# First loads of a sum of a state-space layer and a gated MLP: K tile 0 and x tile 2 moved from ScalarE's DMA queue to SyncE's

## The chip, the cores and the metric

The kernel runs on one core of one Trainium2 chip. The metric is device time in microseconds of one execution. The kernel before takes 177.66 us (median of 3 runs, 177.61 to 177.72).

A core has five engines with instruction queues of their own: TensorE (PE in the profile, its weight loads PEld), VectorE (DVE), ScalarE (ACT), GpSimd (POOL) and SyncE (SP, which here only starts transfers). Transfers between the chip's memory and the on-chip memory are started from the queue of an engine and carried out by 16 DMA engines. Engines wait for each other, and for transfers, by semaphores.

## What is computed

The input x has 2048 rows of 512. A layer norm comes first, then two branches read the normed rows xn, and the output is x plus both:

```python
def _A_ref(x, Lambda_re, Lambda_im, B_re, B_im, C_re, C_im, log_dt, Dskip):
    Lam = Lambda_re + 1j * Lambda_im
    dt = jnp.exp(log_dt)
    Lam_bar = jnp.exp(dt * Lam)
    B_bar = ((Lam_bar - 1.0) / Lam)[:, None] * (B_re + 1j * B_im)
    Bu = jnp.einsum("bld,pd->blp", x + 0j, B_bar)
    for t in range(L):
        h = Lam_bar[None, :] * h + Bu[:, t, :]
    y = 2.0 * jnp.einsum("blp,dp->bld", hseq, Cmat).real + x * Dskip[None, None, :]
def _B_ref(x, w_gate, w_up, w_down):
    return (_silu(x @ w_gate) * (x @ w_up)) @ w_down
xn = _layernorm(x, axis=-1)
return x + _A_ref(xn, ...) + _B_ref(xn, ...)
```

w_gate and w_up are 512 x 1376, w_down is 1376 x 512, B and C are 512 x 512. Everything in memory is bfloat16.

## The kernel before

**Tiling.** The 2048 rows are 16 x tiles of 128 rows, in four chunks of four. The hidden width of 1376 is ten tiles of 128 and a rest of 96; the inner dimension of 512 is four K tiles of 128. For each chunk TensorE computes the gate and up products two hidden tiles at a time (lines 721, 764), ScalarE takes them out of PSUM (silu in line 733, a copy in line 799), and VectorE multiplies them (line 802). TensorE also computes Bu (line 849), VectorE rotates it and runs the recurrence as scans along the rows (lines 880 and 889). At the end come the down product (line 918), the product with C that is added to it (line 932), and an addition on VectorE with the store (line 936). PSUM is used as four pairs of banks, taken in turn.

**The start.** Chunk 0 is normed tile by tile (`ln_chunk0`, lines 514 to 528): statistics of an x tile (518, 519), its standard deviation on ScalarE (520), the reciprocal (525) and the norm (501). All of it is tied into one fixed order on VectorE, and the transpose of the small parameters (523) stands in that order ahead of the reciprocal of tile 3. TensorE transposes each normed tile (549), and ScalarE (560), for tile 3 VectorE (558), moves it to xnT. The first seven hidden tiles of the gate product of chunk 0 are computed in quarters, a quarter being the 128 rows of one x tile, and within a quarter K tile by K tile (line 764, `ffn_gate_quarters`). So seven matmuls need only K tile 0, the next seven K tile 1, and so on. The eighth hidden tile (number 7, `NQ`) follows as a whole in line 775, then the up products.

**The loads.** The first seven hidden tiles of w_gate (896 columns, `FG`) come as four loads, one for each K tile (`wg_load`, 224 KB each); the columns from 896 on come in one load, ld_wg1 (line 442, 480 KB), which hidden tile 7 also needs (`wres`, line 706). w_up comes in two (ld_wu0 and ld_wu1). The x tiles 0 to 3 come singly (`x_load`, 128 KB each), then four at a time. `ld_touch` is a read of 64 bytes. Three parameter rows (`pload`) follow the last single x tile.

**The order.** Work is declared as tasks with reads and writes. A planner (`_schedule`) walks through them with estimated durations and fixes the order of each engine's stream. TensorE's and SyncE's tasks keep the order in which they are declared (`_CHAIN`); ScalarE's, VectorE's and GpSimd's are ordered by the planner's priorities, within extra ordering edges written by hand. For a transfer the planner counts on a rate for each starting queue, which for ScalarE's is half that of SyncE's. A transposing load (`xpose=True`, for instance B_re in line 447) waits for every transfer declared before it, except those named in `beside`, and every later transfer waits for it; so the transfers from ld_bre on follow one another.

**At the top of the queues.** SyncE starts x tiles 0 and 1, K tiles 1, 2, 3, x tile 3, the three parameter rows, then ld_wu0, ld_wg1, ld_wu1 and ld_x4. ScalarE starts ld_touch, K tile 0 and x tile 2, and then loads its activation table with a first small operation, which has an ordering edge behind the last task of `act_q`.

Of the kernel before, what the change touches and what calls it, by code (L numbers as in the profile page):

```python
# [250 lines left out]
def bass_parallel_sum__ssm_conv_s5__swiglu_ffn__prompt_kernel(  # L251
# [32 lines left out]
    with es:  # L284
# [112 lines left out]
        def dma(name, dst, src, writes, nbytes, reads=(), after=(), out_=False, eng="sp", xpose=False, prio=0.0, order=(), beside=(), **kw):  # L397
            after = tuple(after)
            if xpose:
                after = after + tuple(t for t in dma_tasks if t.name not in beside)  # L400
                fn = lambda e, dst=dst, src=src: e.dma_start_transpose(out=dst, in_=src)
                est, nb = 1900.0, int(nbytes * 1.2) + 140000
            else:
                if xp_state[0] is not None:
                    after = after + (xp_state[0],)
                fn = lambda e, dst=dst, src=src: e.dma_start(dst, src, **kw)
                est, nb = 330.0 + nbytes / 900.0, nbytes
            t = g.add(eng, fn, reads=reads, writes=writes, name=name, dma=True, after=after, out=out_, est=est, nbytes=nb, prio=prio, order=order)
            dma_tasks.append(t)
            if xpose:  # L410
                xp_state[0] = t
            return t
# [9 lines left out]
        def x_load(a, **kw):  # L422
            return dma("ld_x%d" % a, x_sb[:, a:a + 1, :], x_v[:, a:a + 1, :], [("x", a)], TILEB, **kw)

        def wg_load(nm, k0, k1, **kw):
            return dma("ld_wg" + nm, wg[:, k0:k1, 0:FG], wg_v[:, k0:k1, 0:FG], [("wg", nm)], (k1 - k0) * 128 * FG * 2, **kw)
# [2 lines left out]
        x_load(0)  # L429
        x_load(1)  # L430
        act_q = [dma("ld_touch", tch[0:16, 0:1], wg_v[0:128:8, 0:1, 0:2], [("tch",)], 16 * 4, eng="act")]
        act_q.append(wg_load("k0", 0, 1, eng="act", order=(act_q[-1],)))
        act_q.append(x_load(2, eng="act", order=(act_q[-1],)))
        wg_load("k1", 1, 2)
        wg_load("k2", 2, 3)
        wg_load("k3", 3, 4)
        x_load(3)
        pload("ld_ldt", 2, A_log_dt)
# [624 lines left out]
```

## Time and profile before

| what | value |
|---|---|
| median of 3 runs | 177.66 us (177.61 to 177.72) |
| the profiled execution, its time | 177.57 us |
| its span, first to last instruction | 175.6 us |
| TensorE matmuls | busy 172.5 us, 98% of the span |
| VectorE | busy 161.5 us, 92% |
| ScalarE | busy 83.3 us, 47% |
| GpSimd | busy 10.6 us, 6% |
| granted TensorE clock | 1.0 throughout |
| DMA | 13.69 MB, 78 GB/s over the span |

The first eight loads, by the timeline of the two queues and the DMA view of each issue alone:

| load | KB | queue | issued at (us) | issue to landing (us) |
|---|---|---|---|---|
| x tile 0 | 128 | SyncE | 0.78 | 2.1 |
| K tile 0 | 224 | ScalarE | 1.23 | 3.2 |
| x tile 2 | 128 | ScalarE | 1.71 | 3.7 |
| K tile 1 | 224 | SyncE | 1.70 | 3.5 |
| K tile 2 | 224 | SyncE | 2.17 | 3.9 |
| K tile 3 | 224 | SyncE | 2.64 | 4.0 |
| x tile 3 | 128 | SyncE | 3.12 | 3.8 |

x tile 1 is the second of the two transfers that SyncE starts from 0.78 us on. Landing is the time at which the last part of a transfer has counted up its semaphore. Times in the views are from the start of the span. A line of the timeline gives the start, the time from the first to the last of the merged instructions, engine, line of the kernel, operation and how many there are; the bracket behind it, if any, is the idle time of the engine before it and what ended it. PEclk, the granted clock, is the third number from the end in the rows of the windows.

### The profile page before, as it was taken

What the parts mean: (1) busy time and instruction counts of PE and PEld (TensorE: products, weight loads), DVE (VectorE), ACT (ScalarE), POOL (GpSimd) and SP (SyncE); (2) the same over time, 40 slices, a digit from 0 to 9 for tenths busy, and PEclk for the clock granted to TensorE, in tenths of its full rate; (3) what the DMA queues carried; (4) which work ended last, traced back from release to release, by engine and by line L of the source; (5) the groups of instructions that cost most, each with busy time, mean ns of one, the idle gap of its engine ahead of it and who ended that gap; (6) DMA issues with size and microseconds to landing.
All of it is one profiled execution on the core that took longest, in us unless ns stands there. A gap on an engine that the chain in (4) does not pass through costs nothing.

```text
span 175.6 us, 2523 instructions
## 1 busy us (share of the span) xinstructions
PE 172.5 (98%) x978; PEld 84.7 (48%) x978; DVE 161.5 (92%) x279; ACT 83.3 (47%) x113; POOL 10.6 (6%) x21
## 2 busy tenths in 40 slices
PE   7899999999999999999999999999999999999995
PEld 2894444444444495444444444444444444444443
DVE  2873999999999999999999999999999999999933
ACT  4479799899999766697560000000265620000000
POOL 3040500217000000000000000000000000000000
DMA  4898665645695102300311000022100000000122
GB/s 161 272 385 186 119 118 168 141 107 101 119 300 117 27 0 60 63 0 13 101 39 28 4 0 0 0 90 93 60 0 0 0 0 0 4 0 0 60 91 90
DMA packets 27143, 13.69 MB, mean 78 GB/s; under 512 B 19356, under 2 KB 27004, under 8 KB 27132
## 3 DMA queue, kind: packets, MB, share of 16 engines
q1 hardware_dynamic: 26812, 13.18, 29.0%
q10 hardware_dynamic: 320, 0.36, 0.6%
q8 instruction: 7, 0.11, 0.3%
q14 instruction: 4, 0.03, 0.1%
HBM read 6.85 MB, written 2.10 MB: 51 GB/s over the span
## 4 chain that ended last, share of the span: by engine, by line
PE 96%; DMA 1%; DVE 1%; ACT 0%; issue 0%
PE pb L721 36%; PE pb L918 20%; PE pb L932 16%; PE pb L849 16%; PE pb L764 4%; PE pb L814 3%; PE pb L957 2%; DMA x_sb<-in_A_x_dram 1%; PE pb L549 1%; DVE st L518 0%; DVE xn_sb L501 0%; ACT xnT L560 0%; DVE x_sb L936 0%; ACT sd L520 0%; DVE mv L519 0%
## 5 line engine op out<-in xcount | busy, mean ns | idle before, releaser
L721 PE MATMUL pb<-xnT,wgu 128*128 128x512 bf16 x212 | 46.2, 379 | 0.0
L889 DVE TENSOR_TENSOR_SCAN rot<-sm,car,rot 128x512 bf16<-128x512 f32 x32 | 39.2, 1267 | 0.1
L733 ACT ACTIVATE sg<-pb 128x1024 bf16<-128x1024 f32 x20 | 20.1, 1021 | 39.5 <-PE pb L721 38.4
L721 PEld LDWEIGHTS pb<-xnT,wgu 128*128 128x128 bf16 x212 | 20.7, 98 | 24.8 <-ACT sg L733 0.2
L932 PE MATMUL pb<-W,hss 128*128 128x512 bf16 (+2 forms) x136 | 28.2, 367 | 0.0
L918 PE MATMUL pb<-wd,hT 128*128 128x512 bf16 (+2 forms) x130 | 26.4, 363 | 0.0
L799 ACT ACTIVATE uf<-pb 128x1024 bf16<-128x1024 f32 x20 | 20.5, 1025 | 6.5 <-PE pb L721 4.9
L849 PE MATMUL pb<-xnT,BT 128*128 128x512 bf16 x96 | 21.0, 379 | 0.0
L932 PEld LDWEIGHTS pb<-W,hss 128*128 128x128 bf16 x136 | 12.7, 98 | 15.3 <-issue 0.8
L918 PEld LDWEIGHTS pb<-wd,hT 128*128 128x128 bf16 x130 | 12.3, 98 | 14.0
L856 ACT ACTIVATE u_sb<-pb 128x1024 bf16<-128x1024 f32 x16 | 16.4, 1024 | 5.5 <-PE pb L849 5.2
L721 PE MATMUL pb<-scrC,wgu 128*128 128x512 bf16 x80 | 17.4, 379 | 0.0
L849 PEld LDWEIGHTS pb<-xnT,BT 128*128 128x128 bf16 x96 | 9.4, 98 | 11.4
L936 DVE TENSOR_TENSOR x_sb<-pb,x_sb 128x512 bf16<-128x512 f32 (+2 forms) x17 | 10.7, 645 | 4.0 <-PE pb L932 4.0
L721 PEld LDWEIGHTS pb<-scrC,wgu 128*128 128x128 bf16 x80 | 7.8, 98 | 9.2
L802 DVE TENSOR_TENSOR hT<-sg,uf 128x1024 bf16<-128x1024 bf16 x15 | 10.1, 681 | 0.1
L485 DVE BATCH_NORM_STATS2 st<-x_sb 128x6 f32<-128x512 bf16 x12 | 7.4, 678 | 2.9 <-DMA x_sb<-in_A_x_dram 2.9
L880 DVE TENSOR_TENSOR rot<-u_sb,cosT 128x2048 bf16<-128x2048 bf16 x8 | 9.8, 1220 | 0.0
L880 DVE TENSOR_TENSOR rot<-u_sb,sin 128x2048 bf16<-128x2048 bf16 x8 | 9.7, 1218 | 0.0
L880 DVE TENSOR_TENSOR rot<-rot,sin 128x2048 bf16<-128x2048 bf16 x8 | 9.7, 1217 | 0.0
L880 DVE TENSOR_TENSOR rot<-rot,cosT 128x2048 bf16<-128x2048 bf16 x8 | 9.7, 1211 | 0.0
L880 DVE TENSOR_TENSOR hss<-rot 128x2048 bf16<-128x2048 bf16 x8 | 9.6, 1218 | 0.0
(85 smaller groups left out, 161.6 us busy)
## 6 DMA issues: line engine op xcount, KB each, us to landing
out_dram<-x_sb SPq DMA_DIRECT2D x15, 128.0 KB, 1.7
x_sb<-in_A_x_dram SPq DMA_DIRECT2D x3, 512.0 KB, 4.6
wd<-in_B_w_down_dram SPq DMA_DIRECT2D x1, 1280.0 KB, 6.4
wgu<-in_B_w_up_dram SPq DMA_DIRECT2D x1, 768.0 KB, 4.7
wgu<-in_B_w_gate_dram SPq DMA_DIRECT2D x3, 224.0 KB, 3.9
wgu<-in_B_w_up_dram SPq DMA_DIRECT2D x1, 608.0 KB, 6.7
wgu<-in_B_w_gate_dram SPq DMA_DIRECT2D x1, 480.0 KB, 5.6
x_sb<-in_A_x_dram SPq DMA_DIRECT2D x3, 128.0 KB, 2.9
```

Source lines behind the costliest of these rows:

```text
L485: return g.add("dve", lambda e, a=a: e.bn_stats(out=st[:, a % 8, :], in_=x_sb[:, a, :]), reads=[("x", a)], writes=[("st", a % 8)], name="b ...
L721: inst = e.matmul(pbank[0:fs, bk, :].rearrange("p (j t) -> p j t", j=4), lhsT=w[:, kt, i * 128:i * 128 + fs], rhs=xnT[c][:, :, kt, :], sta ...
L733: g.add("act", lambda e: e.activation(out=sg[rows, sl, 0:n, :].rearrange("p a t -> p (a t)"), in_=pair_f32(rows, bk, 512 * n), func=AF.Sil ...
L799: g.add("act", lambda e: e.activation(out=uf[rows, ul, 0:n, :].rearrange("p a t -> p (a t)"), in_=pair_f32(rows, bk, 512 * n), func=AF.Ide ...
L802: g.add("dve", lambda e: e.tensor_tensor(out=hT_pair(c, i0), in0=sg[rows, sl, 0:n, :], in1=uf[rows, ul, 0:n, :], op=ALU.mult), reads=[("sg ...
L849: inst = e.matmul(pbank[:, bk, :].rearrange("p (j t) -> p j t", j=4), lhsT=BT[:, ri, kt, pt * 128:(pt + 1) * 128], rhs=xnT[c][:, :, kt, :] ...
L856: g.add("act", lambda e: e.activation(out=u_sb[:, us].rearrange("p r t -> p (r t)"), in_=pair_f32(slice(0, 128), b0), func=AF.Identity), r ...
L880: tt = lambda out, a, b, op, r, w, nm: g.add("dve", lambda e: e.tensor_tensor(out=out, in0=a, in1=b, op=op), reads=r, writes=w, name="%s_% ...
L889: g.add("dve", lambda e, A0=A0, A1=A1, k=k, ri=ri, pt=pt: e.tensor_tensor_scan(out=A1[:, k, ri, :], data0=rr[:, pt:pt + 1].to_broadcast([1 ...
L918: inst = e.matmul(pbank[:, bk, 0:nc_], lhsT=hT_pair(c, i - i % 2)[:, i % 2, lt * 128:(lt + 1) * 128], rhs=wd[:, i, c0:c0 + nc_], start=(i ...
L932: inst = e.matmul(pbank[:, bk, 0:nc_], lhsT=hss[:, hb, pt, ri, lt * 128:(lt + 1) * 128], rhs=W12[:, ri, pt, c0:c0 + nc_], start=False, sto ...
L936: g.add("dve", lambda e: e.tensor_tensor(out=x_sb[:, a, c0:c0 + nc_], in0=pbank[:, bk, 0:nc_], in1=x_sb[:, a, c0:c0 + nc_], op=ALU.add), r ...
```

## The change

K tile 0 and x tile 2 are no longer started by ScalarE, whose queue keeps ld_touch alone. SyncE starts x tiles 0 and 1, K tiles 0, 1 and 2, x tile 2, K tile 3 and x tile 3, one behind the other, and then everything else as before. The ordering edge of ScalarE's table load goes to ld_touch, the last task of `act_q` that is left. Nothing else is edited; sizes, buffers and the work of the other engines are the same, and the planner runs anew over the changed list of tasks.

```diff
         x_load(0)
         x_load(1)
         act_q = [dma("ld_touch", tch[0:16, 0:1], wg_v[0:128:8, 0:1, 0:2], [("tch",)], 16 * 4, eng="act")]
-        act_q.append(wg_load("k0", 0, 1, eng="act", order=(act_q[-1],)))
-        act_q.append(x_load(2, eng="act", order=(act_q[-1],)))
-        wg_load("k1", 1, 2)
-        wg_load("k2", 2, 3)
+        for k in range(3):
+            wg_load("k%d" % k, k, k + 1)
+        x_load(2)
         wg_load("k3", 3, 4)
         x_load(3)
         pload("ld_ldt", 2, A_log_dt)
```

## The prediction

> **What bounds the kernel now.** I read the page's shares first (TensorE busy for 98% of the span, VectorE 92%), then the chain of waits in order of time:
>
> ```profile
> 0.78 2.14 DMA x_sb<-in_A_x_dram
> ...
> 5.39 1.18 PE pb L764 x18
> ...
> 12.62 11.22 PE pb L721 x52
> ...
> 173.02 0.43 PE pb L918 x10
> ```
>
> Columns: start, length, work. The first x tile's transfer, its norm on VectorE and the first transposes end in gate matmuls at 5.39 us; from there to 173.8 us the chain is TensorE almost without a break. So the change can gain little: only what comes ahead of 5.39 us. It can lose wherever a load arrives after the time at which TensorE asks for it, and every such loss reaches the end. As the matmuls stand back to back, two late loads don't add: the end moves by the larger lateness. So I compare each load with its due time.
>
> The timeline of SyncE's queue (start, time taken, transfer):
>
> ```profile
> 0.78 0.87 SPq L406 DMA_DIRECT2D x_sb<-in_A_x_dram  x2
> 1.70 1.38 SPq L406 DMA_DIRECT2D wgu<-in_B_w_gate_dram  x3
> 3.12 0.43 SPq L406 DMA_DIRECT2D x_sb<-in_A_x_dram  x1
> 3.59 0.74 SPq L406 DMA_DIRECT2D prow<-in_A_log_dt_dram  x1
> ...
> 5.54 0.44 SPq L406 DMA_DIRECT2D wgu<-in_B_w_up_dram  x1
> 6.03 0.50 SPq L406 DMA_DIRECT2D wgu<-in_B_w_gate_dram  x1
> ```
>
> Three K tiles take 1.70 to 3.12, so one issue costs 0.47 us of the queue; one x tile 3.12 to 3.59, also 0.47. The transfer at 6.03 is ld_wg1. The DMA issues started around 6.03, taken alone, give its landing (KB, then us):
>
> ```profile
> wgu<-in_B_w_gate_dram SPq DMA_DIRECT2D x1, 480.0 KB, 5.6
> ```
>
> It lands at 11.63. Its first reader is not the fifth gate pair at 18.7 us but `ffn_mm(0, NQ, "g", ...)` in line 775: tile 7 begins at column 896, where the K tiles end. The weight loads on TensorE give its due time:
>
> ```profile
> 12.41 0.58 PEld L721 LDWEIGHTS pb<-xnT,wgu 128*128 128x128 bf16 x4
> ```
>
> These are tile 7's four. It has 12.41 - 11.63 = 0.78 us to spare, the smallest cover on the queue behind the moved issues.
>
> **The two moved issues.** SyncE takes K tile 0 and x tile 2: 2 x 0.47 = 0.94 us more of its queue. K tiles 0, 1, 2 go out at 1.70, 2.17, 2.64, x tile 2 at 3.12, K tile 3 at 3.59, x tile 3 at 4.06, and the three parameter loads, ld_wu0, ld_wg1, ld_wu1 and ld_x4 each 0.94 later. ScalarE's table load starts near 1.25, not 2.19; nothing comes of it, as its first real work (3.89) waits for VectorE.
>
> **The eight first loads.** The windows of DMA (last two columns: share of the engines, GB/s):
>
> ```profile
> 2.42:3.00 0.58, 0.58 (x3) 0.24 (x2) 0.05 (x1) 0.58 (x1) 0.00 (x0) 1.00 0.45 146
> 3.00:5.00 2.00, 1.53 (x10) 0.65 (x9) 1.66 (x5) 0.97 (x3) 0.00 (x0) 1.00 1.03 362
> 5.00:6.20 1.20, 1.11 (x20) 0.88 (x18) 0.86 (x4) 0.92 (x4) 0.00 (x0) 1.00 1.02 383
> 7.20:8.00 0.80, 0.80 (x18) 0.80 (x16) 0.49 (x3) 0.61 (x3) 0.00 (x0) 1.00 0.72 182
> 8.00:9.00 1.00, 1.00 (x22) 0.97 (x19) 0.96 (x4) 0.29 (x3) 0.00 (x0) 1.00 1.01 372
> ```
>
> The engines are full from 3.0 to 6.2 us, and from 5.0 on SyncE's queue alone (q10 has no packet left) fills them at 383 GB/s. I take it that one queue also fills them from 3.0. By 3.0 some 0.22 MB had moved (0.92 us at 144 and 0.58 at 146 GB/s). Going through the new order with 0.131 MB for an x tile and 0.229 for a K tile, the last bytes pass at 3.8 (K0), 4.4, 5.0, 5.4 (x2), 6.0 (K3), 6.3. K tile 3 has the same bytes ahead of it in both kernels and landed at 2.64 + 4.0 = 6.64, so 0.67 after its last byte; adding this to all: K0 4.4, K1 5.1, K2 5.7, x2 6.0, K3 6.64, x3 7.0. Due times: K0 5.39; K1 seven matmuls of 0.056 later (28 take 1.56 in the chain), 5.78; K2 6.17; K3 three matmuls after the weights at 6.56, 6.73; x2 6.35 (third BATCH_NORM_STATS2); x3 8.06. All are in time, K3 by 0.09 us only. Cost 0. If the queue fills the engines later, K3 pays first. Upper bound: between 2.42 and 2.98 the queue delivered 68 packets, which would make 1.05 us of each tile, against 271 packets per us in 5.0 to 6.2; I take the latter, nearest in load.
>
> **ld_wg1.** 0.94 later is 12.57, and a wait's end reaches the weight load 0.05 later (xn_sb ends at 4.74, TensorE starts at 4.79): 12.62 - 12.41 = 0.21 us of wait. Bounds: what precedes ld_wg1 on the engines is ld_wu0, which starts slowly: 39 GB/s from 6.6 to 7.2, 182 to 8.0, then 372. The 0.17 MB moved by 8.0 are worth 0.46 us at full rate, so it runs as if full from 7.54, 2.0 us after its issue. Likewise x tiles 8 to 11 (issued 27.37; 92 GB/s from 28.4 to 29.0, then 370) come to 1.48 us, and w_down (issued 47.35) to 1.77. With 1.48 instead of 2.0, ld_wg1 lands at 12.05 and nothing waits. I take 2.0: the same transfer after the same pause. On the far side, were each added issue as slow as the 0.74 us at 3.59, it lands 0.53 later: 0.74 us of wait.
>
> A rule of the Trainium skill goes against this term. "DMA: Bandwidth & Descriptors", section "Issuing engines are not separate DMA queues", says that transfers started from several engines share the same 16 DMA engines, so that a second starter saves only issue time, usually small beside the transfer. By the rule the sum would be 0, as in the first rival. The trace agrees that 0.94 us is small beside 5.6, but not beside a cover of 0.78.
>
> **The rest of the queue.** ld_wu0 lands at 5.54 + 4.7 = 10.24, then 11.2; its matmuls follow tile 7's. The parameter loads' landings aren't shown; the last is issued at 4.97, then 5.91, its transpose due at 8.89. At the 2.0 us of the small read on ScalarE's queue it has 1 us left; a later one would hold xn3 and the transposes at 10.06. ld_wu1 lands at 6.58 + 6.7 = 13.28, and the transpose load of B_re waits for it (issue 13.29, 4.6 us), then B_im (17.95, 4.3 us, landing 22.3). B_im's weights are due four matmuls after those at 23.47: 24.33. With 0.94 more it lands at 23.2, 1.1 us in hand. ld_x4 lands at 15.98 and VectorE, idle for 2.94 us, starts on it at 16.00:
>
> ```profile
> 16.00 2.47 DVE L485 BATCH_NORM_STATS2 st<-x_sb 128x6 f32<-128x512 bf16 x4 [2.94 <-DMA x_sb<-in_A_x_dram]
> ...
> 157.79 2.35 DVE L880 TENSOR_TENSOR hss<-rot 128x2048 bf16<-128x2048 bf16 x2
> ```
>
> From there it has no idle time until 167 us, so all its work moves 0.94. The last hss pair is ready at 160.14, then 161.1; its first reader follows 32 matmuls of 0.216 after 159.42, at 166.3. VectorE's idle ends near the end (0.99, 1.04, 1.03 us) take up the rest. In the middle, hmul0_0 (18.67) queues behind these statistics and releases ScalarE's buffer for the copy at 19.41, done at 20.43; its PSUM bank is due at 23.85. Cost 0, with 2.4 us or more in hand each. The planner may reorder VectorE and ScalarE a little, as its transfer times move too; the same covers pay.
>
> **Sum.** 0.21 us at line 775, nothing else: 177.57 (profiled: 175.6 of span and 1.97 around it) + 0.21 = 177.78. The median of the runs, 177.66, is 0.09 above the profiled execution, so I forecast 177.87. About 0.2% (0.36 us) is what a measurement of this kernel can tell from no change; the forecast is inside it.
>
> **The rivals.**
> - ld_wg1 in time: ld_wu0 starts up as the loads at 27 and 47 us did, because its first slow stretch belonged to the moment. 177.66. Against it: that stretch is this very transfer's.
> - Slower, one queue doesn't keep the first stage fed or keep its pace: K tile 3, x tile 2 or ld_wg1 land 0.4 to 0.9 us after their due times. It decides from 6.73 us for K3 (cover 0.09), 12.41 for ld_wg1. For it: 146 GB/s between 2.42 and 3.0 with queued work; against: 383 GB/s later. Middle 0.65: 178.3.
> - Slower by the transposes: ld_x4's landing takes 8.9 us, though the engines fall from 356 GB/s (12.6 to 13.8) to 73 (13.8 to 14.5): a last piece straggled some 1.5 us. If in the new time that hits ld_wu1, B_re starts at 13.29 + 0.94 + 1.5 = 15.7 and B_im lands at 24.7 against 24.33: 0.4 us, 178.06.
> - Faster: x tile 0, freed of ScalarE's transfers, lands sooner; the 128 KB stores take 1.7 us against its 2.14, so up to 0.44. It pays only if ld_wg1 is in time as well: 12.05 + 0.05 leaves 0.31 of it, 177.35. Against: K tile 0 was issued 0.45 us after x tile 0, and nearly all traffic on ScalarE's queue falls after 2.92.
>
> **How the numbers follow.** Chances: forecast 0.42, ld_wg1 in time 0.14, the first stage or the queue's pace 0.22, the transposes 0.14, faster 0.08. Within 0.2%: the rival in time and most (0.34) of the forecast's case, 0.48. Slower: 0.08 of the forecast's own spread up to 0.74, 0.22 and 0.14, 0.44. Faster 0.08. The likeliest case alone spans 177.7 to 178.4; the range 177.5 to 178.5 leaves out most of the faster case and the first stage's worst.
>
> **What would show it.** Right: the weight load of line 721 after the gate quarters starts near 12.6, with idle time ended by the w_gate transfer; SyncE issues ld_wu0 at 6.48; TensorE starts on L764 at 5.39 still; ld_x4 lands near 16.9. Wrong: idle time of TensorE at 6.7 (K3) or 24.3 (B_im), first matmuls away from 5.39, or tile 7 on time.

## The result, and the profile after

| kernel | median of its runs | lowest to highest | runs |
|---|---|---|---|
| before | 177.61 us | 177.42 to 178.23 | 17 |
| after | 178.38 us | 177.75 to 178.87 | 17 |

The ratio is 1.0042, 95% interval 1.0033 to 1.0052: the change costs 0.75 us, more than the 0.2% that can be told from nothing. The forecast was 177.87 us and the range 177.5 to 178.5, so the range holds the median, but the likeliest case is not what happened: the case of the first stage (second rival, middle 178.3) is. The range held because that rival was in it, not by the sum. The profiled execution of the changed kernel took 178.41 us, with a span of 176.6 us (175.6 before), at a granted clock of 1.0.

The chain of waits of the changed kernel (start, length, work), which before went back to the first x tile:

```profile
3.59 4.16 DMA wgu<-in_B_w_gate_dram
7.75 0.05 issue
7.80 0.73 PE pb L763 x10
...
13.65 11.22 PE pb L720 x52
24.87 13.81 PE pb L848 x64
```

(The line numbers of the changed kernel are smaller by 1.) The chain now goes back to a weight load: K tile 3, issued at 3.59, landed at 7.75. Before, line 721's 52 matmuls began at 12.62 in this view, now at 13.65: 1.03 us later, and the span is 1.0 longer. So all of this execution's loss is there before 8 us, and nothing behind it changes it.

The timeline of TensorE's weight loads in the changed kernel (the bracket is idle time before the group and what ended it):

```profile
5.42 0.95 PEld L763 LDWEIGHTS pb<-xnT,wgu 128*128 128x128 bf16 x14 [0.20 <-ACT xnT L559]
6.87 0.24 PEld L763 LDWEIGHTS pb<-xnT,wgu 128*128 128x128 bf16 x4 [0.50 <-issue]
...
7.79 0.56 PEld L763 LDWEIGHTS pb<-xnT,wgu 128*128 128x128 bf16 x10 [0.41 <-DMA wgu<-in_B_w_gate_dram]
```

The gate matmuls start at 5.42 (5.39 before). After 14 of them, seven for each of K tiles 0 and 1, TensorE is idle for 0.50 us, and again for 0.41 us before the first that needs K tile 3. The trace puts the first gap down to "issue"; the matmul side of the same stop (6.90) names the load of w_gate. Together 0.91 of the 1.0 us (the matmul side, whose ends are modelled, counts 0.35 and 0.24).

How long the loads took, from the view of the DMA issues, each taken alone (KB, then us from issue to landing): K tile 2 (issued 2.65), x tile 2 (3.12) and K tile 3 (3.59).

```profile
wgu<-in_B_w_gate_dram SPq DMA_DIRECT2D x1, 224.0 KB, 4.1
x_sb<-in_A_x_dram SPq DMA_DIRECT2D x1, 128.0 KB, 4.0
wgu<-in_B_w_gate_dram SPq DMA_DIRECT2D x1, 224.0 KB, 4.2
```

| load | due (prediction) | landing forecast | measured | late |
|---|---|---|---|---|
| K tile 1 | 5.78 | 5.1 | 4.9 | no |
| K tile 2 | 6.17 | 5.7 | 6.76 | 0.6 |
| x tile 2 | 6.35 | 6.0 | 7.16 | 0.8 |
| K tile 3 | 6.73 | 6.64 | 7.75 | 1.0 |

The issue times are those of the forecast to 0.01 us. It is the transfers that are late. The windows (the last two columns: busy share of the DMA engines, GB/s), first of the kernel before, then of the changed one:

```profile
3.00:3.60 0.60, 0.60 (x3) 0.20 (x2) 0.60 (x1) 0.59 (x2) 0.00 (x0) 1.00 1.01 356
3.60:4.40 0.80, 0.73 (x4) 0.25 (x2) 0.46 (x4) 0.38 (x2) 0.00 (x0) 1.00 1.01 356
4.40:5.80 1.40, 0.91 (x13) 0.69 (x14) 1.12 (x3) 0.65 (x4) 0.00 (x0) 1.00 1.05 381
```

```profile
2.42:3.00 0.58, 0.58 (x3) 0.24 (x2) 0.08 (x1) 0.39 (x2) 0.00 (x0) 1.00 0.90 258
3.00:3.60 0.60, 0.60 (x3) 0.20 (x2) 0.60 (x1) 0.00 (x0) 0.00 (x0) 1.00 0.78 245
3.60:4.40 0.80, 0.80 (x4) 0.29 (x2) 0.46 (x4) 0.20 (x1) 0.00 (x0) 1.00 1.01 365
4.40:5.80 1.40, 1.24 (x11) 0.83 (x10) 1.09 (x3) 0.66 (x4) 0.00 (x0) 1.00 0.82 195
```

With the 146 GB/s that the prediction shows for 2.42 to 3.0 us, the kernel before moved 0.58 MB from 2.42 to 4.4 us and the changed one 0.59 MB: it is ahead in the first window, behind in the second and level at 4.4 us. The loss is made from 4.4 to 5.8 us, where it moves 1.4 x (381 - 195) = 0.26 MB less. At 380 GB/s that is 0.7 of the 1.1 us by which K tile 3 lands later (7.75, 6.67 before); these rows don't account for the rest. The landings show the same place: K tile 1 lands 0.3 us sooner than before, K tile 2 only 1.85 us after it (0.8 before), and x tile 2 and K tile 3 again 0.4 and 0.6 us apart.

### The profile page after: what moved, and what is told of

It reads as the page before. It is cut to its first block, busy times and chain, and to the rows that moved or that the text cites. A ratio compares the mean times of both kernels' runs of the same rounds, so it can differ in the third digit from the quotient of the medians.

```text
span 176.6 us, 2516 instructions
## 1 busy us (share of the span) xinstructions
PE 172.6 (98%) x970; PEld 85.2 (48%) x978; DVE 161.7 (92%) x279; ACT 83.4 (47%) x113; POOL 10.2 (6%) x21
## 4 chain that ended last, share of the span: by engine, by line
PE 94%; DMA 2%; SPq 1%; issue 1%; DVE 0%
PE pb L720 36%; PE pb L917 19%; PE pb L848 16%; PE pb L931 16%; PE pb L763 3%; PE pb L813 3%; DMA wgu<-in_B_w_gate_dram 2%; PE pb L956 2%; SPq L406 1%; PE pb L548 0%; DVE x_sb L935 0%; PE pb L928 0%
## 5 line engine op out<-in xcount | busy, mean ns | idle before, releaser
L931 PE MATMUL pb<-W,hss 128*128 128x512 bf16 (+2 forms) x132 | 27.6, 366 | 0.4 <-issue 0.3
L879 DVE TENSOR_TENSOR rot<-rot 128x2048 bf16<-128x2048 bf16 x8 | 9.6, 1216 | 0.0
```

The costliest lines, as they stand in the source:

```text
L879: tt = lambda out, a, b, op, r, w, nm: g.add("dve", lambda e: e.tensor_tensor(out=out, in0=a, in1=b, op=op), reads=r, writes=w, name="%s_% ...
L931: inst = e.matmul(pbank[:, bk, 0:nc_], lhsT=hss[:, hb, pt, ri, lt * 128:(lt + 1) * 128], rhs=W12[:, ri, pt, c0:c0 + nc_], start=False, sto ...
```

## The experiments

Two explanations had to be told apart. The first: one queue with all eight loads starves the first stage (theory A). The second: the moved issues delay everything behind them on SyncE's queue, and some cover there breaks. The planner's new order is a third suspect: by the traces at least 79 positions on VectorE and 24 on ScalarE hold another instruction than before. Here is what each run gave in the windows from 3.0 to 3.6 and 4.4 to 5.8 us, as profiled; the ratio is to the kernel before on the same chip. "On ScalarE" is what ScalarE's queue carries of the eight loads. One execution of each kernel is profiled: those of x2_on_sp (177.35 us), slots_only (178.12) and merged (178.86) are the shortest or nearly the shortest of their runs, so their rows show less than the ratio does.

| kernel | on ScalarE | GB/s 3.0 to 3.6 / 4.4 to 5.8 | K tile 3 landed | ratio (95%) |
|---|---|---|---|---|
| before | K0, x2 | 356 / 381 | 6.67 | |
| after | none | 245 / 195 | 7.75 | 1.0042 (1.0033 to 1.0052) |
| after_again | none | 181 / 238 | 8.19 | one run |
| after_params_pool | none | 115 / 264 | 7.92 | 1.0055 (1.0041 to 1.0069) |
| after_old_order | none | 234 / 234 | 8.22 | 1.0057 (1.0043 to 1.0071) |
| touch_all | none | 191 / 237 | 7.96 | 1.0040 (1.0023 to 1.0057) |
| merged | none | 239 / 240 | 7.68 | 1.0110 (1.0076 to 1.0145) |
| k0_on_sp | x2 | 314 / 316 | 7.52 | 1.0033 (1.0021 to 1.0045) |
| x2_on_sp | K0 | 368 / 361 | 6.67 | 1.0016 (1.0005 to 1.0027) |
| k1_on_act | K1 | 378 / 329 | 7.00 | 1.0016 (1.0000 to 1.0033) |
| slots_only | K0, x2 | 362 / 390 | 6.84 | 1.0054 (1.0037 to 1.0071) |
| slots_old_order | K0, x2 | 342 / 377 | 7.03 | 1.0032 (1.0017 to 1.0046) |
| before_params_pool | K0, x2 | 356 / 345 | 7.25 | 1.0014 (1.0004 to 1.0023) |
| k0_k2_on_act | K0, K2 | 360 / 363 | 6.59 | 0.9997 (0.9986 to 1.0007) |

The 6.67 of the kernel before is the trace's time; the prediction's 6.64 is added up from rounded rows. The edits of slots_only, k0_on_sp, x2_on_sp, slots_old_order, before_params_pool and k0_k2_on_act are against the kernel before, the others against the changed kernel.

**after_again** is the changed kernel once more: is the slow first stage a chance of one execution?

> The changed kernel once more, for a second profile. Theory A (one queue leaves the DMA engines badly used in 4.4 to 5.8 us: 195 GB/s at a share of 0.82, against 381 at 1.05 before): the loss is there again, below 300 GB/s in that stretch, K tile 2 lands after 6.2 and K tile 3 after 7.0, so TensorE waits on line 763 for over 0.3 us and the span is 176.2 to 176.8. Rival B (a chance hold-up of the memory in that one execution): K tile 3 lands by 6.7 as worked out in the prediction, and what is left is a wait of some 0.2 us for the columns from 896 on: span 175.8.

It took 178.87 us in its one run, span 177.1. TensorE waited 0.38 and 0.23 us for w_gate, K tile 2 landed at 7.21. It is no chance; the loss was larger still.

**slots_only** takes the change's other half alone: the kernel before, with two 64-byte reads into an unused tile at the place where SyncE's queue is lengthened.

```diff
         x_load(3)
+        for n in range(2):
+            dma("ld_slot%d" % n, tch[0:16, 2 + n:3 + n], wg_v[0:128:8, 0:1, 0:2], [("slot", n)], 16 * 4)
```

> The queues as before, and two reads of 64 bytes behind x tile 3 on SyncE's queue, so that the parameter loads and the four big loads behind them go out 0.94 us later and the first eight loads don't change. The term of the prediction by itself: ld_wg1 lands at 12.4 to 12.6 against 12.41 and TensorE waits 0 to 0.2 us: 177.6 to 177.9, ratio 1.000 to 1.001. Theory A expects the same, as the first stage is untouched. Rival C (all of the loss is the later issue of what stands behind, by the transposing loads or by VectorE's later start): the full 0.7 us, 178.3.

178.64 us, +1.0 us: a miss, as it was to cost 0.2 at most. The first stage is almost as before (362 and 390 GB/s, the gate matmuls 0.11 us late). Tile 7 starts late as the prediction's sum said: ld_wg1 lands at 12.62, the weights start at 12.66 where 12.41 was due; 0.14 of these 0.25 us is the wait for ld_wg1. The rest comes later. The chain of waits of slots_only:

```profile
7.53 7.87 DMA wgu<-in_B_w_up_dram
15.42 4.54 DMA BT<-in_A_B_re_dram
19.97 4.06 DMA BT<-in_A_B_im_dram
24.05 6.17 DMA xnT<-xn_sb
...
30.24 3.59 DMA x_sb<-in_A_x_dram
...
33.85 2.47 DVE st L487 x4
...
45.88 0.92 ACT uf L801
46.80 0.05 issue
46.84 1.25 PE pb L723 x5
```

ld_wu1 took 7.87 us (6.7 before) and landed at 15.40. B_re, B_im and the transposing load of xn, which took 6.17 us (4.7 before), follow one another, then x tiles 8 to 11 land at 33.83. Before, they had landed at 30.84, and VectorE began on them at 31.24. So they are 3.0 us late, not 0.94: the two long loads make most of it. That cover of 0.4 us is not in the prediction. VectorE now starts at 33.85 after 1.78 us of idle time; ScalarE's sine, its copies and the norms behind it slip, and TensorE waits for ScalarE's copy of a PSUM bank, as its timeline shows:

```profile
46.84 8.81 PE L723 MATMUL pb<-xnT,wgu 128*128 128x512 bf16 x40 [0.34 <-ACT uf L801]
```

So the later start of tile 7 (0.25) and this wait (0.34) add up to most of the 0.7 us by which this execution's span grew (176.3).

**k0_on_sp** and **x2_on_sp** move one of the two loads each.

```diff
...
-        act_q.append(wg_load("k0", 0, 1, eng="act", order=(act_q[-1],)))
         act_q.append(x_load(2, eng="act", order=(act_q[-1],)))
-        wg_load("k1", 1, 2)
-        wg_load("k2", 2, 3)
-        wg_load("k3", 3, 4)
+        for k in range(4):
+            wg_load("k%d" % k, k, k + 1)
```

> K tile 0 alone on SyncE's queue, x tile 2 stays on ScalarE's: from 4 us on two queues still carry loads until x tile 2 is through. Theory A in the form that the engines need a second queue: x tile 2 lands by 5.4 and VectorE isn't held; K tiles 2 and 3 are still almost alone on their queue and land some tenths late: 177.8 to 178.2. Rival C (issue slots): half of the loss, about 177.9 to 178.0. Rival D (the loss needs x tile 2's small pieces between the K tiles): 177.6 to 177.7.

178.19 us. With K tile 0 alone moved, K tile 1 lands at 6.34 and TensorE stops for it. Its timeline in k0_on_sp:

```profile
6.47 0.95 PE L762 MATMUL pb<-xnT,wgu 128*128 128x128 bf16 x11 [0.50 <-DMA wgu<-in_B_w_gate_dram]
```

```diff
         act_q.append(wg_load("k0", 0, 1, eng="act", order=(act_q[-1],)))
-        act_q.append(x_load(2, eng="act", order=(act_q[-1],)))
         wg_load("k1", 1, 2)
         wg_load("k2", 2, 3)
+        x_load(2)
```

> x tile 2 alone on SyncE's queue between K tiles 2 and 3, K tile 0 stays on ScalarE's. ScalarE's queue is empty from about 4.1 us on, so by theory A the stretch of 4.4 to 5.8 us is as badly used as in the changed kernel, K tile 3 lands after 6.9: 178.0 to 178.4. If it is well used (over 350 GB/s), what counts is how full the queue is when that stretch begins, not that there is one queue: then K tile 3 lands by 6.7 and x tile 2 by 6.3, 177.6 to 177.8.

177.91 us. In the profiled execution, the shortest of its runs, no load of the first stage is late (K tile 2 at 5.62, x tile 2 at 6.08, K tile 3 at 6.67). The two queue rows of the DMA view between 4.4 and 5.8 us (packets, MB, the packets' time as a share of 16 engines) say most. First x2_on_sp, then the changed kernel:

```profile
q1 hardware_dynamic: 378, 0.51, 97.6%
```

```profile
q1 hardware_dynamic: 207, 0.27, 82.2%
```

In both, SyncE's queue (q1) is the only one with packets in that stretch, and work is waiting in it. In the one it moves 378 packets, in the other 207. A packet takes 0.976 x 16 x 1.4 / 378 = 58 ns in the one, 0.822 x 16 x 1.4 / 207 = 89 ns in the other, where the engines also stand idle for a fifth of the stretch. So one queue can fill the engines here; it does not when K tile 0 has gone through it too. What the median of x2_on_sp loses (0.3 us) this profile doesn't show.

**after_params_pool** takes the three parameter loads off SyncE's queue in the changed kernel (GpSimd starts them), so that SyncE issues ld_wu0 at 4.56 us, sooner than either kernel (5.54 before, 6.49 after): this more than undoes the added slots and leaves the order of the first stage as changed.

```diff
         x_load(3)
-        pload("ld_ldt", 2, A_log_dt)
-        pload("ld_lim", 1, A_Lambda_im)
-        pload("ld_lre", 0, A_Lambda_re)
...
+        pload("ld_ldt", 2, A_log_dt, eng="pool", order=pool_first)
+        pload("ld_lim", 1, A_Lambda_im, eng="pool", order=pool_first)
+        pload("ld_lre", 0, A_Lambda_re, eng="pool", order=pool_first)
```

> The changed kernel with the three parameter loads started from GpSimd's queue instead: the first eight loads stay one behind the other on SyncE's queue, but ld_wu0, ld_wg1, ld_wu1 and ld_x4 go out some 0.9 us earlier than before the change, not 0.94 later. Theory A (the first stage by itself makes the loss): the engines are badly used between 4.4 and 5.8 us again, K tile 3 lands after 7.0, 178.1 to 178.5. Rival C (the later issue behind it makes the loss): 177.5 to 177.7. Rival E (the parameter loads, issued from 4.54 to 6.45 us in the changed kernel, are what breaks into that stretch): over 350 GB/s there, K tile 3 by 6.7, 177.5 to 177.7; the profile tells C from E.

178.59 us: no cure. K tile 3 is issued at 3.61 and lands at 7.92. The first stage alone is enough for the loss, and the parameter loads' place in SyncE's queue is not what disturbs it. The slow stretch lies earlier here (115 GB/s from 3.0 to 3.6 us; K tile 0 lands at 5.50, in the changed kernel at 4.37), while GpSimd issues its loads, so this run's first stage is not quite the changed kernel's. By the traces VectorE's order differs in 5 positions from that of before.

**slots_old_order** is slots_only with the planner counting the two reads as no time, which gives each engine exactly the order of before.

```diff
+        for n in range(2):
+            dma("ld_slot%d" % n, tch[0:16, 2 + n:3 + n], wg_v[0:128:8, 0:1, 0:2], [("slot", n)], 0).est = 0.0
```

> The two small reads on SyncE's queue once more, but the planner counts them as nothing, so that every engine has the order of the kernel before. The real shift by itself: ld_wg1 0.2 us late and the transposing chain with ld_x8 behind it late. If the planner's new order made the second wait in the run without this (46.84 us), 177.7 to 177.9. If the late chain made it whatever the order, 178.4 to 178.7 as there.

178.19 us (+0.5), between what the two sides expected: late loads cost something whatever the order. Whether the rest of slots_only's loss belongs to the new order is not shown, as the intervals overlap. The profiled execution was a long one of this kernel (178.66), and its waits are not quite the same. K tiles 2 and 3 land at 6.44 and 7.03, so tile 7 starts 0.30 us late without waiting for ld_wg1 (12.44). B_im lands at 25.02, and its weights on TensorE wait for it:

```profile
25.07 1.84 PEld L851 LDWEIGHTS pb<-xnT,BT 128*128 128x128 bf16 x10 [0.55 <-DMA BT<-in_A_B_im_dram]
```

That moves the matmuls by 0.2 us. Then ld_wu1 at 15.38 and x tiles 8 to 11 at 34.51 lead to a stop of 0.41 us at 47.24, on the same copy as in slots_only.

**after_old_order** gives the changed kernel the orders of before on VectorE, ScalarE and GpSimd, written out by name.

```diff
+        for eng_, order_ in _OLD.items():
+            row = [left[(eng_, nm)].pop(0) for nm in order_]
+            for t_, u_ in zip(row, row[1:]):
+                u_.od.add(t_)
```

> The changed kernel with ScalarE's, VectorE's and GpSimd's streams in the order of the kernel before. Theory A: the loss is made ahead of 8 us, where both orders are the same, so 178.2 to 178.5. Rival F (the planner's new order makes the loss): 177.6 to 177.9.

178.74 us. TensorE's stop for K tile 2 grows to 0.99 us at 7.39, so this execution starved a little more, and the order is not the cause.

**merged** asks whether each load costs something of its own: in the changed kernel, K tiles 2 and 3 come as one load behind x tile 2.

```diff
-        for k in range(3):
+        for k in range(2):
...
-        wg_load("k3", 3, 4)
+        dma("ld_wgk23", wg[:, 2:4, 0:FG], wg_v[:, 2:4, 0:FG], [("wg", "k2"), ("wg", "k3")], 2 * 128 * FG * 2)
```

> One queue still, but K tiles 2 and 3 as one load and x tile 2 ahead of it: seven loads for eight, the same bytes. If each load costs the queue some 0.7 us however large (seven of eight end by 7.2 in the two profiles of the changed kernel), K tiles 2 and 3 land near 6.9 and x tile 2 near 5.7: 177.8 to 178.1. If the pieces or the bytes are what one queue brings slowly, both K tiles land at 7.7: 178.3 to 178.9, as TensorE now waits for both at 6.2.

179.28 us, or 179.08 for the four of its six runs with a granted clock of 1.0 (0.99 in the other two), so the ratio overstates it. The pair lands at 7.68, about where K tile 3 did, and now K tile 2 waits with it: one stop of 1.33 us, at 7.73. With one load fewer in the queue, the rate between 4.4 and 5.8 us is still 240 GB/s. It is not a price per load.

**k1_on_act** has K tile 1 instead of K tile 0 on ScalarE's queue.

```diff
-        for k in range(3):
-            wg_load("k%d" % k, k, k + 1)
+        act_q.append(wg_load("k1", 1, 2, eng="act", order=(act_q[-1],)))
+        wg_load("k0", 0, 1)
+        wg_load("k2", 2, 3)
```

> The changed kernel with K tile 1, not K tile 0, on ScalarE's queue: SyncE's has seven first loads, as in the run with x tile 2 alone moved, and begins its w_gate loads with K tile 0. Theory A1 (what counts is that 0.23 MB run on the other queue early, whichever tile): the stretch of 4.4 to 5.8 us above 350 GB/s, K tile 3 by 6.8, 177.8 to 178.0, as with K tile 0 there. Rival G (the queue that reads the first K tile after the small read on the other queue is slowed for it): as with K tile 0 alone moved, 300 GB/s or less, 178.1 to 178.4.

177.83 us. K tile 2 is in time, and K tile 3 holds up the weight loads for 0.26 us, where the two stops of the changed kernel were 0.91 in all. TensorE's weight loads in k1_on_act:

```profile
7.04 0.56 PEld L764 LDWEIGHTS pb<-xnT,wgu 128*128 128x128 bf16 x10 [0.26 <-DMA wgu<-in_B_w_gate_dram]
```

So it is not K tile 0 that matters: another K tile on the second queue cures most of it too.

**touch_all** widens the small early read to rows of all four K tiles, in case the first access to a part of w_gate is slow.

```diff
-        act_q = [dma("ld_touch", tch[0:16, 0:1], wg_v[0:128:8, 0:1, 0:2], [("tch",)], 16 * 4, eng="act")]
+        act_q = [dma("ld_touch", tch[0:16, 0:4], wg_v[0:128:8, 0:4, 0:2], [("tch",)], 64 * 4, eng="act")]
```

> The changed kernel with the small read widened from K tile 0 to all four K tiles (64 pieces of 4 bytes for 16). Rival G2 (the slow stretches are first reads of parts of w_gate that the small read hasn't touched): 3.0 to 3.6 and 4.4 to 5.8 us above 340 GB/s, K tile 3 by 6.8, 177.6 to 177.9. Theory A: nothing changes, below 300 GB/s there, K tile 3 after 7.2, 178.2 to 178.6.

178.42 us, 191 and 237 GB/s: no first-access cost is seen.

**before_params_pool** makes the edit of after_params_pool in the kernel before: does a shorter SyncE queue gain?

> The kernel before with the three parameter loads on GpSimd's queue, so that ld_wu0, ld_wg1, ld_wu1 and ld_x4 go out 1.9 us earlier and all covers behind them grow by as much. TensorE's chain was without a break from 5.39 us on in the profile of before, so by theory A the profiled time is the same and only executions in which a cover failed gain: 177.4 to 177.6, ratio 0.998 to 1.000. Rival: the big loads, started earlier, now run beside K tiles 2 and 3 and x tile 3 and hold them: 177.8 to 178.3.

177.92 us, ratio 1.0014: a little slower. ld_wu0 and ld_wg1 are now issued right behind the first loads, and GpSimd's parameter loads run beside those; TensorE's timeline shows K tile 3 late:

```profile
7.29 0.73 PE L766 MATMUL pb<-xnT,wgu 128*128 128x128 bf16 x10 [0.40 <-DMA wgu<-in_B_w_gate_dram]
```

**k0_k2_on_act** exchanges K tile 2 and x tile 2 between the queues of the kernel before, so that no issue slot moves.

```diff
-        act_q.append(x_load(2, eng="act", order=(act_q[-1],)))
+        act_q.append(wg_load("k2", 2, 3, eng="act", order=(act_q[-1],)))
         wg_load("k1", 1, 2)
-        wg_load("k2", 2, 3)
+        x_load(2)
```

> The kernel before with K tile 2 and x tile 2 exchanged between the queues: ScalarE's carries K tiles 0 and 2 (0.46 MB, 0.36 before), SyncE's x tiles 0 and 1, K tile 1, x tile 2, K tile 3, x tile 3, so neither queue has one issue more or less and nothing behind them moves. Theory A1 (the more evenly the first bytes lie on both queues, the better the engines are used): K tile 3 lands by 6.5, the covers of K tiles 2 and 3 grow, 177.4 to 177.6, ratio 0.998 to 1.000. Rival: the part of each queue is of no account once 0.2 MB run on the other, and the order alone counts: K tile 2, now behind K tile 0 on one queue, lands when it did, ratio 0.999 to 1.001. Against both: over 177.9 if any departure from the order of before costs.

177.52 us, beside 177.68 of the kernel before: ratio 0.9997, interval 0.9986 to 1.0007, no difference. No version beat the kernel before.

## Why the prediction was right or wrong

**What bounds the kernel, and latenesses that don't add: right.** Behind 7.8 us the chain is TensorE to the end, and the lateness of K tile 3 (1.0) is the growth of the span (1.0).

**"The two moved issues": right.** Issues in steps of 0.47, ld_wu0 at 6.49, ld_wg1 at 6.98. Nothing came of the earlier table load. Of the prediction's signs, the first gate matmuls came in time (5.42) and ld_wu0's issue too; tile 7 started at 13.43, not near 12.6, and TensorE idles before 6.87, which it had named as a sign of being wrong.

**"The eight first loads": this is the step that failed.** It read "I take it that one queue also fills them from 3.0", from 383 GB/s that SyncE's queue reached alone between 5.0 and 6.2 us, and set the cost at 0 with 0.09 us in hand. In the changed kernel the one queue does fill them from 3.6 to 4.4 us (365 GB/s), but from 4.4 to 5.8 us it brings 195 GB/s, and K tile 3 is 1.0 us late. Six profiles of kernels with all four K tiles and x tile 2 on that queue show 115 to 245 GB/s between 3.0 and 3.6 and 195 to 264 between 4.4 and 5.8 us. With a K tile on ScalarE's queue they show 342 to 378 and 329 to 390. The row read was true, but of a queue that didn't carry K tile 0: x2_on_sp shows the same rate (361) from the same queue in the same place, and only K tile 0's way in differs. The other bound that the prediction had in hand, 68 packets between 2.42 and 2.98 us, was the nearer one for that stretch: the changed kernel's 207 packets in 1.4 us are 148 per us, nearer to that 121 than to 271. The second rival had this mechanism with its place (K tile 3 from 6.73) and a middle of 178.3, against 178.38 measured; with 0.09 us in hand and two bounds so far apart, its chance of 0.22 was too small.

**"ld_wg1", 0.21 us: right in itself, but not on the path.** It landed at 12.39 (12.57 forecast), and in the changed kernel tile 7 asks for it only at 13.43. Where the first stage is nearly on time, in slots_only, tile 7 starts 0.25 us late, which is the size of the term, though 0.11 of it comes from the first stage.

**"The rest of the queue", cost 0: wrong, and hidden here.** The list of covers has ld_wu1, B_re, B_im and ld_x4, but leaves out what follows them in the same order: the transposing load of xn and x tiles 8 to 11, whose 0.4 us is the smallest cover of that chain. The slots alone cost 0.5 us (slots_old_order, 1.0017 to 1.0046) to 1.0 us (slots_only). The third rival had ld_wu1's last piece 1.5 us late with a landing near 15.7; it landed at 15.40 there. But that rival let it out through B_im's weights, and there it comes out through VectorE and ScalarE at 46.8 us. In slots_old_order it comes out both ways, 0.2 us at B_im's weights and 0.41 us at 47.2. In the profiled execution of the changed kernel ld_wu1 landed at 14.20, x tiles 8 to 11 at 31.47, and TensorE, 1 us late itself, didn't wait.

**The Trainium skill's rule.** "DMA: Bandwidth & Descriptors", section "Issuing engines are not separate DMA queues", has a second starter save only issue time. The runs here differ: the rate between 4.4 and 5.8 us is 195 to 264 GB/s in the six profiles with one starter and 329 to 390 in the seven with a K tile on a second. The times agree but don't decide it: k0_on_sp and x2_on_sp move one load each and so the same issue time, and stand at 1.0033 and 1.0016, with intervals that overlap. And the issue time, small beside a transfer, is not small beside a cover, as slots_only shows.

**The faster rival fell**: x tile 0 landed at 2.89 us, 2.92 before, though ScalarE's queue was empty beside it. The planner's new order, costed at nothing, is not the loss of the changed kernel (after_old_order); whether it matters in slots_only is open.

**What stays open.** The pieces of a queue that carries all four K tiles take longer, and engines stand idle while it has work. In four of the six profiles the gap lies between the landings of K tiles 1 and 2 (1.8 to 2.3 us), behind the queue's fourth load. It is not the number of loads, a first access, the parameter loads' place or the engines' orders. Whether it is the number of pieces waiting in the queue, or how fast the queue is read behind its first loads, no run tells. How often ld_wu1 straggles isn't known either: the two profiles with the slots show it, and those of touch_all (15.82) and merged (15.09); that of the changed kernel doesn't.

## What to carry to other kernels

A rate read from a queue while a second one carries part of the burst is not the rate of that queue with the whole burst: here the one queue gave 365 GB/s from 3.6 to 4.4 us and 195 from there to 5.8. If two queues feed a first stage whose loads have 0.1 us to spare, cost the move to one queue by the poorest row of that queue too, not by the best alone. When loads move back on a queue, follow the chain of loads behind it to its end, through every engine that works in order, and write down the smallest cover of each; a cover of 0.4 us two engines away decided in slots_only. One run of each half of a change shows what the whole hides, since a late first stage covers a late second one.

## What the runs showed of the hardware

- The first loads (128 to 224 KB, 448 KB in merged) on SyncE's queue alone keep the 16 DMA engines at 195 to 264 GB/s in the stretch from 4.4 to 5.8 us; with K tile 0 or 1 started from ScalarE's queue they run at 329 to 390. A packet took 89 ns in the changed kernel, 58 ns in x2_on_sp. It is not the rate of one queue as such: from 3.6 to 4.4 us the changed kernel's ran at 365 GB/s.
- The last part of a load can come late while nearly all engines are idle. The DMA view of slots_only between 13.4 and 15.4 us (40 slices of 0.05 us: busy share of the engines in tenths, and the rate) ends at about a tenth of the rate, a share of 0.07 from 15.2 to 15.4 us, about what one engine of the 16 makes, while the load of w_up isn't complete:

```profile
DMA  9999999999989999999999999999877543210100
GB/s 325 366 338 392 343 323 332 389 369 410 328 307 369 389 389 369 328 352 348 389 352 369 393 307 307 348 307 266 266 205 246 164 123 102 62 41 20 41 20 20
```

- Starting the later loads earlier is no gain by itself: in before_params_pool K tile 3 landed at 7.25 instead of 6.67 us. GpSimd's parameter loads moved in that stretch too, and no run tells which of the two delayed it.
- TensorE's first gate matmuls can come at half the pace, at a granted clock of 1.00. In the profiled execution of k0_k2_on_act (177.95 us, median 177.52) seven of them are 0.106 us apart instead of 0.056. Their weight loads in the kernel before, then there:

```profile
5.39 1.01 PEld L764 LDWEIGHTS pb<-xnT,wgu 128*128 128x128 bf16 x18 [0.32 <-ACT xnT L560]
```

```profile
5.46 1.41 PEld L764 LDWEIGHTS pb<-xnT,wgu 128*128 128x128 bf16 x18 [0.21 <-ACT xnT L560]
```

Every first load of that execution is in time, and its span is 0.4 us longer (176.0). So two single profiles can differ by 0.4 us without any load being late. In the changed kernel's profile some of the first matmuls are slow as well, but the wait for K tile 2 hides it.
